# The order of a chunk's queries in the scores, and the gate of a batch's last 64 tokens on GpSimd

## The chip, the cores and the metric

One core of one Trainium2 chip. The time is device microseconds of one execution; before the change the median of three runs is 2122.11 us (2121.88 to 2122.24).

The engines, as the profile names them: PE is TensorE (matmuls; PEld its weight loads), DVE is VectorE, ACT is ScalarE, POOL is GpSimd, SP is SyncE, which issues the transfers.

## The reference

For each of 8 batches of 3136 tokens: scores of z with itself, rectified and squared, times v, gated by u; then of every batch the 128 tokens with the highest score against `w_gate` go through a small network (256 to 1024 to 256) and are added back with a sigmoid gate.

```python
scale = 1.0 / S                                       # S = 3136
scores = scale * np.matmul(z, z.transpose(0, 2, 1))   # z: 8 x 3136 x 64
attn = np.maximum(scores, 0.0) ** 2
x = u * np.matmul(attn, v)                            # u, v: 8 x 3136 x 256
gates = np.einsum('bsd,d->bs', x, w_gate)
top_idx = np.argpartition(-gates[b], capacity)[:capacity]       # capacity = 128
ye = np.maximum(xe @ w1, 0.0) @ w2
out[b, top_idx] = x[b, top_idx] + g[:, None] * ye               # g = sigmoid of the gate
```

## The kernel before

Everything is float32. To keep its precision on TensorE, an operand is split in a high part (rounded to fp32r) and a low part (the rest), and a product is high by high, high by low and low by high.

**Tiling.** A batch is cut in chunks of 512 queries (`CH`; six whole ones, `WHOLE`, and 64 tokens that are left, `REST`) and in tiles of 128 keys (`P`). A *slot* is a chunk with a pair of key tiles; slots of a batch and the batches stand one behind the other. For a new slot TensorE computes the scores (`scores`, L857): for each of the two key tiles a matmul with weights from `ZH` and one with weights from `ZL`, both with the moving operand `Z`, the chunk's 512 queries (high parts in partitions 0 to 63, low parts in 64 to 127). The result is the PSUM tile `sc`, in one of two rings. ACT rectifies it into `a` (`rise`) and squares it into the high part `hi` (`high`); VectorE or ACT squares `a` itself (`square`, and with that `sc` is free), and GpSimd or VectorE takes the low part `lo` = `a` - `hi` (`low`). Then `hi` and `lo` are the moving operands of the products with `V` (`multiply`), 8 matmuls with `hi` and 4 with `lo` in a slot, which add up in two PSUM banks of the chunk, `acc`, out of three.

**Symmetry.** Scores are symmetric, so a pair of a chunk and an earlier chunk's keys isn't computed again. VectorE transposes `a` in blocks of 32 x 32 (`turn`, `turn_own`), SyncE stores it in `squares` in HBM, and later fetches it into `qk` (`fetch`). Such an *old* slot (`old_scores`, L769) needs only a copy of the high part on ACT and the low part on GpSimd or VectorE. The slot on a chunk's diagonal takes half its columns from `own` (`half`, `fetch_own`), and its second score is 256 columns wide.

**The order of queries.** `ZH` and `ZL` hold z by tiles of 128 keys, in which the 512 tokens of a chunk stand as (t f a): t of 4 tiles, f of 4 groups, a of 32 tokens. The moving operand of the scores is the same data read as (f t a), so that it goes over the chunk in the order of its tokens: 16 runs of 32 elements, in the order of a view, not of memory:

```python
if c < WHOLE:
    Z[b, c] = t.rearrange("p (t f a) -> p f t a", t=GT, a=Q)
```

**A chunk's end.** When a chunk's last product is done, VectorE multiplies each accumulator by u (`evict` in `finish`) into `ut`, transposes it into `x`, SyncE stores it, GpSimd multiplies it by the gate weights and VectorE adds up the gates. The 64 tokens left over (`finish_rest`, L1208) end a batch: ACT and VectorE add three quarters of an accumulator in the tile `xr` (`lower`, `upper`, `total`), GpSimd multiplies by u (`product`), and VectorE weighs 2 x 32 tokens by the gate weights `w_bc` and adds the products up in one instruction each (`weigh`, `gate_of`, output `junk`).

**What sets the order.** The program is straight-line. While it is built, a planner with a clock model of each engine (`Clock`, `advance`, `choices`) puts the next piece of work on an engine: a `job` names the engines that may take it (`"pool|dve"`), a rank and what it needs. TensorE takes scores, then steps of the routing, then products, of what the model says is ready. So a change of a job's shape or engine moves instructions on all engines.

Of the kernel before, what the change touches and what calls it, by code (L numbers as in the profile page):

```python
# [18 lines left out]
P = 128  # L19
CH = 512  # L20
GT = 4
# [260 lines left out]
def attention_then_routed_ffn(ctx: ExitStack, tc: tile.TileContext, zt, ut, v, wg, w1, w2, cst, cst16, keys, outs, at, cap):  # L282
# [323 lines left out]
    def bring_z(b, c):  # L606

        c0, w = CHUNKS[c]
        t = moving_ring.take("Z", F32R)
        Z[b, c] = t[:, :w]  # L610
        for rows, z in ((slice(0, 64), ZH), (slice(64, P), ZL)):
            nc.sync.dma_start(t[rows, :w].bitcast(F32), z[rows, c0 : c0 + w].bitcast(F32))
        if c < WHOLE:
            Z[b, c] = t.rearrange("p (t f a) -> p f t a", t=GT, a=Q)

    def first_z():

        t = moving_ring.take("Z", F32R)
        Z[0, 0] = t.rearrange("p (t f a) -> p f t a", t=GT, a=Q)
# [129 lines left out]
    def fetch_own(b, c):  # L749
        ring = z_ring if c == 0 else v_ring  # L750
        st = ring.take("own", uses=2)
# [17 lines left out]
    def old_scores(k):  # L769
        b, c, js, _ = slots[k]  # L770
        g, t = js[0] // GT, js[0] % GT
        by = lambda x: x.rearrange("p q (f a) -> p q f a", a=Q)
        st = {}

        def high(e):
            src = fetched[b, c, g]
            st["src"] = src[:, :, t * Q : (t + 2) * Q].rearrange("p f (q a) -> p q f a", a=Q)
# [4 lines left out]
            job("pool|dve", k + 0.1, low, [st["src"], hi], [lo_ring], lambda: near(k), takes(2 * CH))  # L782

        def low(e):
            lo = lo_ring.take("lo", F32R)
            rest_on(e, by(lo), st["src"], by(parts[k][0]))
            parts[k][1], parts[k][3] = lo, True
            for _ in range(2):
                old_ring.drop(fetched[b, c, g])
# [31 lines left out]
    def own_rest(k, ps):  # L821
# [3 lines left out]
        def rise(e):  # L825
            a_.append(a_ring.take("a"))
            nc.scalar.activation(a_[0][:REST, 0, :REST], ps[:REST, 0, :REST], AF.Relu)
            job("act", k, high, [a_[0][:REST, 0, :REST]], (), lambda: "own_rest" in consts)

        def high(e):  # L830
            a = a_[0][:REST, 0, :REST]
            st = consts["own_rest"]
            nc.scalar.activation(st[:REST, :REST], a, AF.Square)
# [23 lines left out]
    def scores(k):  # L857
# [3 lines left out]
        if is_second(k):  # L861
            mov, w = mov[:, :, 2:], w // 2
# [15 lines left out]
        def rise(e):  # L878
            st["a_"] = a_ring.take("a")
            st["a"] = st["a_"][:, :n, :w]  # L880
            nc.scalar.activation(st["a"], ps, AF.Relu)
            job("act", k, high, [st["a"]], [hi_ring], lambda: near(k))

        def high(e):
# [5 lines left out]
            by = lambda x: x.rearrange("p q (f x) -> p q f x", x=P)  # L890
            if second:
                st["pieces"] = [(lambda x: by(x)[..., 64:], a.rearrange("p q (f x) -> p q f x", x=64))]
                nc.scalar.activation(st["pieces"][0][0](hi), st["pieces"][0][1], AF.Square)
# [7 lines left out]
        def half(e):  # L901
            src, ring, tile_ = fetched[b, c, c]
            hi = parts[k][0]
            by = lambda x: x.rearrange("p q (f x) -> p q f x", x=P)
            view = lambda x: by(x)[..., :64]
            src = src.rearrange("p f (q x) -> p q f x", q=2)
# [3 lines left out]
            job("pool|dve", k + 0.1, lambda e: low(e, view, src, lambda: ring.drop(tile_)), [src, view(hi)], took=takes(CH), rings=room, ok=turn_of)  # L910

        def square(e):
            a = st["a"]
            if e == "act":
                nc.scalar.activation(a, a, AF.Square)
# [22 lines left out]
        def low(e, view, src, after):  # L938
            if "lo" not in st:
                st["lo"] = lo_ring.take("lo", F32R)  # L940
                st["lows"] = 2 if second else 1
# [12 lines left out]
        def turn(q):  # L954
# [5 lines left out]
            nc.vector.transpose(to, a[rows, q].rearrange("p (m t a) -> p m t a", t=GT, a=Q))  # L960
# [25 lines left out]
        def turn_own(q):  # L986
# [5 lines left out]
            nc.vector.transpose(to, a[:, q].rearrange("p (m t a) -> p m t a", t=GT, a=Q)[:, :, 2:])  # L992
# [109 lines left out]
    def finish(b, c, h):  # L1102
# [106 lines left out]
    def finish_rest(b):  # L1209
# [14 lines left out]
        def upper(e):  # L1224
            s = st["s"]
            nc.vector.tensor_scalar(s, bank[:REST, D:], SCALE * SCALE, None, op0=ALU.mult)
            nc.vector.scalar_tensor_tensor(s, bank[:REST, :D], SCALE * SCALE, s, op0=ALU.mult, op1=ALU.add)
            drop_bank(bank)
            job("dve", rank + 2, total, [st["l"], s])

        def total(e):
            nc.vector.scalar_tensor_tensor(st["s"], st["l"], SCALE * SCALE, st["s"], op0=ALU.mult, op1=ALU.add)
# [993 lines left out]
```

## Time and profile before

| | us |
|---|---|
| median of 3 runs | 2122.11 |
| the profiled execution, its own time | 2121.96 |
| its span in the trace | 2119.8 |
| TensorE busy (matmuls) | 2090.4 (99%) |
| VectorE, ScalarE, GpSimd busy | 1387.1, 1346.5, 1374.7 (64 to 65%) |

The span is what the trace covers from the first instruction to the last; 2.2 us of the execution lie around it. Matmuls are pipelined: the record of one lasts some 390 ns, and the next begins after some 230, so the pace is read from the starts. The timeline view puts equal instructions that follow each other in one row, with the time of the first start.

### The profile page before, as it was taken

To read this page: it belongs to the slowest core of one execution; us is meant where nothing else is said; L and a number is where in the kernel's file an instruction comes from. 1 tells how busy PE (TensorE), PEld (TensorE's weight loads), DVE (VectorE), ACT (ScalarE), POOL (GpSimd) and SP (SyncE) were. 2 spreads that over 40 slices of the span, in tenths; PEclk is the share of its full clock that TensorE was granted. 3 is DMA by queue.
4 is the path that set the end of the run, shared out by engine and by line. 5 is a ranking of instruction groups with operands and counts; after the bars stand their busy time and mean duration, and the time that the engine had idled before them with its cause. 6 is when DMAs were issued, how large, how long until landed. Compare 5 with 4: busy or idle time off the path is not lost.

```text
span 2119.8 us, 28812 instructions
## 1 busy us (share of the span) xinstructions
PE 2090.4 (99%) x9317; PEld 1681.6 (79%) x9317; DVE 1387.1 (65%) x2216; ACT 1346.5 (64%) x1574; POOL 1374.7 (65%) x652
## 2 busy tenths in 40 slices
PE   8999999999999999999999999999999999999998
PEld 6888777887778877788777887778877888777777
DVE  6764587545875458754687446774467764787785
ACT  7766567655776557765676656766566665766642
POOL 6566766568665677656776568665676657755652
PEclk9999999999999999999999999999999999999999
DMA  7799667886678766787677876778767768667763
GB/s 212 213 256 256 171 189 207 248 214 168 184 215 252 206 159 204 222 255 195 159 202 218 263 185 171 201 222 253 185 172 207 205 180 198 182 194 198 213 156 93
DMA packets 426150, 428.37 MB, mean 202 GB/s; under 512 B 129040, under 2 KB 329360, under 8 KB 422416
## 3 DMA queue, kind: packets, MB, share of 16 engines
q1 hardware_dynamic: 425008, 424.18, 73.1%
q0 software_dynamic: 768, 2.10, 0.3%
q8 instruction: 73, 1.20, 0.2%
q14 instruction: 77, 0.63, 0.1%
q10 hardware_dynamic: 224, 0.26, 0.0%
HBM read 238.47 MB, written 175.37 MB: 195 GB/s over the span
## 4 chain that ended last, share of the span: by engine, by line
PE 69%; DMA 10%; SPq 6%; DVE 6%; issue 6%; ACT 2%; POOL 1%; POOLq 0%; ACTq 0%; DVEq 0%
PE acc L206 55%; PE sc L206 11%; SPq L206 6%; DMA squares<-aT 3%; DMA qk<-squares 2%; DMA squares_own<-aT 2%; DVE aT L206 2%; DMA vst<-in_v 2%; ACT hi L206 1%; DVE a L206 1%; DVE rest_hl L206 1%; ACT a L206 1%; PE y L206 1%; PE h L206 1%; DVE lo L206 1%
## 5 line engine op out<-in xcount | busy, mean ns | idle before, releaser
L206 PE MATMUL acc<-hi,V 128*128 128x512 f32 x4800 | 1226.4, 393 | 6.8 <-ACT hi L206 4.6
L206 PEld LDWEIGHTS acc<-hi,V 128*128 128x128 f32 x4800 | 893.1, 188 | 201.1 <-ACT hi L206 8.7
L206 POOL TENSOR_TENSOR lo<-a,hi 128x1024 fp32r<-128x1024 f32 (+1 forms) x243 | 584.4, 2406 | 389.1 <-ACT a L206 270.6
L206 PE MATMUL acc<-lo,V 128*128 128x512 f32 x2304 | 636.4, 393 | 0.0
L206 DVE STREAM_TRANSPOSE aT<-a 128x512 f32<-128x512 f32 (+2 forms) x622 | 381.4, 647 | 296.4 <-ACT a L206 204.1
L206 ACT ACTIVATE a<-sc 128x1024 f32<-128x1024 f32 (+1 forms) x392 | 353.9, 903 | 257.3 <-PE sc L206 71.8
L206 PEld LDWEIGHTS acc<-lo,V 128*128 128x128 f32 x2304 | 429.3, 188 | 91.5 <-POOL lo L206 2.6
L206 POOL TENSOR_TENSOR lo<-qk,hi 128x1024 fp32r<-128x1024 f32 x166 | 416.3, 2508 | 105.4 <-ACT hi L206 88.2
L206 ACT ACTIVATE hi<-a 128x1024 fp32r<-128x1024 f32 (+1 forms) x384 | 366.4, 955 | 153.1 <-PE acc L206 137.2
L206 ACT CAST hi<-qk 128x1024 fp32r<-128x1024 f32 x240 | 250.8, 1048 | 190.6 <-PE acc L206 157.7
L206 PE MATMUL sc<-Z,ZH 128*128 128x512 f32 (+1 forms) x728 | 280.1, 388 | 13.7 <-DVE a L206 9.8
L206 PE MATMUL sc<-Z,ZL 128*128 128x512 f32 (+1 forms) x728 | 275.1, 381 | 0.6 <-POOL ZL L206 0.6
L206 ACT ACTIVATE a<-a 128x1024 f32<-128x1024 f32 x237 | 251.4, 1061 | 6.7
L206 DVE TENSOR_TENSOR a<-sc,a 128x1024 f32<-128x1024 f32 (+3 forms) x155 | 129.9, 838 | 99.9 <-ACT hi L206 77.9
L206 PEld LDWEIGHTS sc<-Z,ZH 128*128 128x128 f32 x728 | 136.9, 188 | 57.2 <-DVE a L206 18.1
L206 DVE TENSOR_TENSOR lo<-a,hi 128x1024 fp32r<-128x1024 f32 (+1 forms) x93 | 141.1, 1518 | 32.5 <-ACT a L206 28.3
L206 PEld LDWEIGHTS sc<-Z,ZL 128*128 128x128 f32 x728 | 138.2, 190 | 29.7 <-POOL ZL L206 0.9
L206 POOL TENSOR_TENSOR ut<-x,w_run 128x1024 f32<-128x1024 f32 x45 | 129.6, 2881 | 34.0 <-DVE x L206 34.0
L206 DVE TENSOR_TENSOR lo<-qk,hi 128x1024 fp32r<-128x1024 f32 x74 | 132.4, 1789 | 21.4 <-ACT hi L206 14.7
L206 POOL TENSOR_TENSOR V<-vst,V 128x512 fp32r<-128x512 f32 (+1 forms) x67 | 85.7, 1285 | 75.9 <-ACT V L206 75.4
L206 DVE SCALAR_TENSOR_TENSOR ut<-acc,ut 128x512 f32<-128x512 f32 x96 | 63.4, 681 | 77.5 <-PE acc L206 77.2
L206 DVE TENSOR_TENSOR V<-vst,V 128x512 fp32r<-128x512 f32 x37 | 57.5, 1569 | 51.1 <-ACT V L206 51.1
(195 smaller groups left out, 1163.5 us busy)
## 6 DMA issues: line engine op xcount, KB each, us to landing
squares<-aT SPq DMA_DIRECT2D x240, 512.0 KB, 4.5
qk<-squares SPq DMA_DIRECT2D x480, 256.0 KB, 6.1
ut<-in_ut SPq DMA_DIRECT2D x48, 512.0 KB, 5.4
vst<-in_v SPq DMA_DIRECT2D x191, 128.0 KB, 3.3
out<-x SPq DMA_DIRECT2D x188, 128.0 KB, 3.6
squares_own<-aT SPq DMA_DIRECT2D x47, 256.0 KB, 2.0
own<-squares_own SPq DMA_DIRECT2D x188, 64.0 KB, 3.1
zst<-in_zt SPq DMA_DIRECT2D x85, 128.0 KB, 6.8
```

The source lines that it names most:

```text
L206: got = real(*args, **kw)
```

## The change

The scores' moving operand is read as it lies, in the order of z's key tiles (`bring_z`, `first_z`). All that comes from scores is then in the order (t f a), and it is put back where it is used otherwise: the transposes read `a` in the other order (`turn`, `turn_own`), old slots and the diagonal's half put the fetched columns in the new order, and the eviction reads the accumulator through a view. The second score of the diagonal takes the last 256 columns as one run. The low part of an old slot is taken in two instructions of 512 columns (`for q in range(2)`), the diagonal's in two of 256.

The factor `SCALE * SCALE` of the eviction moves into the relu, and the squares get `1 / SCALE`.

For the last 64 tokens, `total` and `product` go to GpSimd, `weigh` becomes one product of 64 x 256 on GpSimd, and VectorE adds up 2 x 32 tokens (`add`). The last batch keeps its own way for this (`column`).

```diff
@@ bring_z, first_z
-        if c < WHOLE:
-            Z[b, c] = t.rearrange("p (t f a) -> p f t a", t=GT, a=Q)
-        Z[0, 0] = t.rearrange("p (t f a) -> p f t a", t=GT, a=Q)
+        Z[0, 0] = t
@@ old_scores
+            st["left"] = 2
+            for q in range(2):
+                room = lambda: () if parts[k][1] else (lo_ring,)
+                job("pool|dve", k + 0.1, lambda e, q=q: low(e, q), [st["src"], hi], room, lambda: parts[k][1] or near(k), takes(CH))
-            job("pool|dve", k + 0.1, low, [st["src"], hi], [lo_ring], lambda: near(k), takes(2 * CH))
@@ scores
-            mov, w = mov[:, :, 2:], w // 2
+            mov, w = mov[:, w // 2 :], w // 2
-            nc.scalar.activation(st["a"], ps, AF.Relu)
+            nc.scalar.activation(st["a"], ps, AF.Relu, scale=SCALE * SCALE)
-                nc.scalar.activation(hi, a, AF.Square)
+                nc.scalar.activation(hi, a, AF.Square, scale=1 / SCALE)
@@ half
+            for q in range(2):
+                job("pool|dve", k + 0.1, lambda e, q=q: low(e, lambda x: view(x)[:, q], src[:, q], lambda: ring.drop(tile_)), [src, view(hi)], took=takes(CH // 2), rings=room, ok=turn_of)
@@ turn
-            nc.vector.transpose(to, a[rows, q].rearrange("p (m t a) -> p m t a", t=GT, a=Q))
+            nc.vector.transpose(to, a[rows, q].rearrange("p (t m a) -> p m t a", t=GT, a=Q))
@@ finish: evict
-            nc.vector.scalar_tensor_tensor(
-                xT[:, h], acc[b, c, h], SCALE * SCALE, xT[:, h], op0=ALU.mult, op1=ALU.mult
-            )
+            to, src = xT[:, h], acc[b, c, h]
+            if c < WHOLE:
+                to = to.rearrange("p (f t a) -> p f t a", t=GT, a=Q)
+                src = src.rearrange("p (t f a) -> p f t a", t=GT, a=Q)
+            nc.vector.tensor_tensor(to, src, to, op=ALU.mult)
@@ finish_rest
-            job("dve", rank + 2, total, [st["l"], s])
+            job("pool" if scored else "dve", rank + 2, total, [st["l"], s])
-            job("pool|dve" if scored else "dve", rank + 2, product, [st["s"]], took=takes(D), ok=lambda: b in turned_u)
+            job("pool" if scored else "dve", rank + 2, product, [st["s"]], ok=lambda: b in turned_u)
-                for i in range(2):
-                    job("dve", rank + 6, lambda e, i=i: weigh(i), [st["x"]])
+                job("pool", rank + 6, weigh, [st["x"]])
-        def weigh(i):
+        def weigh(e):
+            nc.gpsimd.tensor_tensor(st["s"], st["x"], consts["wg"][:REST], op=ALU.mult)
+            for i in range(2):
+                job("dve", rank + 8, lambda e, i=i: add(i), [st["s"]])
+
+        def add(i):
-            gate_of(st["x"][at_], gate[b][at_, o : o + 1], at_)
+            nc.vector.tensor_reduce(gate[b][at_, o : o + 1], st["s"][at_], axis=AX.X, op=ALU.add)
```

VectorE at the end of the second batch, from the first instruction on `xr` on. Before (`junk` is the gate product, `a<-sc,a` the square that frees a score bank, `ut<-acc,ut` the eviction):

```order
L206 TENSOR_SCALAR xr<-acc 64x256
L206 SCALAR_TENSOR_TENSOR xr<-acc,xr 64x256
L206 SCALAR_TENSOR_TENSOR xr<-xr 64x256
L206 TENSOR_TENSOR lo<-qk,hi 128x1024
L206 SCALAR_TENSOR_TENSOR junk,gate<-xr,w_bc 32x256
L206 TENSOR_TENSOR V<-vst,V 128x512
L206 SCALAR_TENSOR_TENSOR junk,gate<-xr,w_bc 32x256
L206 STREAM_TRANSPOSE aT<-a 128x8x32 x2
L206 TENSOR_TENSOR a<-sc,a 128x1024
L206 SCALAR_TENSOR_TENSOR ut<-acc,ut 128x512
```

And now:

```order
L206 COPY xr<-acc 64x256
L206 TENSOR_TENSOR xr<-acc,xr 64x256
L206 TENSOR_TENSOR lo<-qk,hi 128x512 x3
L206 TENSOR_TENSOR ZL<-zst,ZH 128x4x4x32
L206 TENSOR_TENSOR V<-vst,V 128x512
L206 STREAM_TRANSPOSE aT<-a 128x8x32 x2
L206 TENSOR_TENSOR ut<-acc,ut 128x512
L206 TENSOR_TENSOR lo<-a,hi 128x1024
L206 TENSOR_TENSOR ut<-acc,ut 128x512
L206 STREAM_TRANSPOSE aT<-a 128x4x128 x2
L206 TENSOR_REDUCE gate<-xr 32x1
```

The two gate products are gone from ahead of the square and the eviction; three halves of `lo<-qk` and a `ZL` stand there, and the first sum of the gate comes behind the evictions.

GpSimd at the same place. Before:

```order
L206 TENSOR_TENSOR rest_hl<-rest,rest_hl 128x8x64
L206 TENSOR_TENSOR lo<-a,hi 128x8x64
L206 TENSOR_TENSOR xr<-xr,rest_u 64x2x4x32
L206 TENSOR_TENSOR lo<-qk,hi 128x1024
L206 TENSOR_TENSOR ZL<-zst,ZH 128x4x4x32
L206 TENSOR_TENSOR V<-vst,V 128x512
L206 TENSOR_TENSOR lo<-a,hi 128x1024
```

And now:

```order
L206 TENSOR_TENSOR rest_hl<-rest,rest_hl 128x8x64
L206 TENSOR_TENSOR lo<-a,hi 128x2x256
L206 TENSOR_TENSOR xr<-xr 64x256
L206 TENSOR_TENSOR lo<-qk,hi 128x512
L206 TENSOR_TENSOR lo<-own,hi 128x256 x2
L206 TENSOR_TENSOR xr<-xr,rest_u 64x2x4x32
L206 TENSOR_TENSOR V<-vst,V 128x512
L206 TENSOR_TENSOR lo<-a,hi 128x1024
L206 TENSOR_TENSOR xr<-xr,w_bc 64x256
```

Two instructions on `xr` are new there, and three stand in a chain with other work between them.

TensorE at the same place, from the last two matmuls of the new chunk's second score to the third score. Before:

```order
L206 MATMUL sc<-Z,ZH 128x512
L206 MATMUL sc<-Z,ZL 128x512
L206 MATMUL acc<-hi,V 128x512 x8
L206 MATMUL acc<-lo,V 128x512 x4
L206 MATMUL sc<-Z,ZH 128x512
```

And now:

```order
L206 MATMUL sc<-Z,ZH 128x512
L206 MATMUL sc<-Z,ZL 128x512
L206 MATMUL acc<-lo,V 128x512 x4
L206 MATMUL sc<-Z,ZH 128x512
L206 MATMUL sc<-Z,ZL 128x512
```

The third score follows the second after 4 products in place of 12; between the third and the fourth there are 12 in both.

In the whole program, instructions that take the low part, by engine:

| | GpSimd before | now | VectorE before | now |
|---|---|---|---|---|
| `lo<-qk`, 1024 columns | 166 | 0 | 74 | 0 |
| `lo<-qk`, 512 columns | 0 | 261 | 0 | 219 |
| `lo<-a`, 1024 columns | 228 | 199 | 61 | 90 |

## Rows read from the trace of the kernel before

**Rows 1.** The page: the span, and each engine's busy time and share.

```profile
span 2119.8 us, 28812 instructions
...
PE 2090.4 (99%) x9317; PEld 1681.6 (79%) x9317; DVE 1387.1 (65%) x2216; ACT 1346.5 (64%) x1574; POOL 1374.7 (65%) x652
```

**Rows 2.** TensorE's groups by shape: xcount | busy us, mean ns | idle us.

```profile
L206 PE MATMUL acc<-hi,V 128*128 128x512 f32 x4800 | 1226.4, 393 | 6.8 <-ACT hi L206 4.6 <-DVE hi L206 1.9
L206 PE MATMUL sc<-Z,ZH 128*128 128x512 f32 x626 | 254.0, 406 | 13.7 <-DVE a L206 9.8 <-ACT a L206 3.4 <-DVE Z L206 0.5
L206 PE MATMUL sc<-Z,ZL 128*128 128x512 f32 x626 | 248.5, 397 | 0.6 <-POOL ZL L206 0.6
...
L206 PE MATMUL h<-wl,xh 128*128 128x512 f32 x24 | 7.5, 395 | 0.0
```

**Rows 3.** Timeline, TensorE, 1001 to 1012 us: start us, us, instruction, xcount.

```profile
1001.71 1.98 PE L206 MATMUL acc<-hi,V 128*128 128x512 f32 x8
1003.52 1.08 PE L206 MATMUL acc<-lo,V 128*128 128x512 f32 x4
...
1008.58 0.40 PE L206 MATMUL sc<-Z,ZH 128*128 128x512 f32 x1
...
1009.52 1.99 PE L206 MATMUL acc<-hi,V 128*128 128x512 f32 x8
1011.35 0.84 PE L206 MATMUL acc<-lo,V 128*128 128x512 f32 x3
```

**Rows 4.** Timeline of TensorE where an expert's first layer runs, 416 to 418 us.

```profile
416.31 0.62 PE L206 MATMUL h<-wh,xh 128*128 128x512 f32 x2
...
417.70 1.09 PE L206 MATMUL acc<-hi,V 128*128 128x512 f32 x4
```

**Rows 5.** Waits of TensorE: us in total, times, longest us.

```profile
PE sc L206 <- DVE a L206: 9.8, 14, 1.1
```

**Rows 6.** VectorE's groups by shape: the last 64 tokens' gate.

```profile
L206 DVE SCALAR_TENSOR_TENSOR junk<-xr,w_bc 32x256 f32<-32x256 f32 x14 | 53.3, 3808 | 4.6 <-POOL xr L206 4.4
```

**Rows 7.** Timeline of all engines at the second batch's end, 519 to 530 us.

```profile
519.36 5.11 DVE L206 SCALAR_TENSOR_TENSOR junk<-xr,w_bc 32x256 f32<-32x256 f32 x1 [0.64 <-POOL xr L206]
...
524.21 3.15 POOL L206 TENSOR_TENSOR lo<-a,hi 128x1024 fp32r<-128x1024 f32 x1
524.48 1.06 ACT L206 ACTIVATE hi<-a 128x1024 fp32r<-128x1024 f32 x1
...
525.12 2.52 DVE L206 SCALAR_TENSOR_TENSOR junk<-xr,w_bc 32x256 f32<-32x256 f32 x1
...
527.88 0.61 PE L206 MATMUL acc<-lo,V 128*128 128x512 f32 x2
...
528.35 1.19 DVE L206 TENSOR_TENSOR a<-sc,a 128x1024 f32<-128x1024 f32 x1
...
529.59 0.50 PE L206 MATMUL sc<-Z,ZH 128*128 128x512 f32 x1 [1.10 <-DVE a L206]
```

**Rows 8.** Groups by line and shape, VectorE (DVE), then GpSimd (POOL).

```profile
L206 DVE TENSOR_TENSOR lo<-qk,hi 128x1024 fp32r<-128x1024 f32 x74 | 132.4, 1789 | 21.4 <-ACT hi L206 14.7 <-DMA qk<-squares 3.6 <-issue 2.9
L206 DVE TENSOR_TENSOR lo<-a,hi 128x1024 fp32r<-128x1024 f32 x61 | 94.7, 1553 | 29.6 <-ACT a L206 28.3 <-issue 1.1
L206 DVE SCALAR_TENSOR_TENSOR ut<-acc,ut 128x512 f32<-128x512 f32 x96 | 63.4, 681 | 77.5 <-PE acc L206 77.2
...
L206 DVE TENSOR_REDUCE gate<-ut 128x16 f32<-128x1024 f32 x45 | 54.3, 1207 | 42.0 <-POOL ut L206 42.0
L206 DVE TENSOR_TENSOR lo<-a,hi 128x512 fp32r<-128x512 f32 x32 | 46.4, 1451 | 2.9
...
L206 DVE TENSOR_TENSOR a<-sc,a 128x512 f32<-128x512 f32 x47 | 32.2, 686 | 55.7 <-ACT hi L206 55.2 <-issue 0.5
...
L206 POOL TENSOR_TENSOR xr<-xr,rest_u 64x256 f32<-64x256 f32 x7 | 11.6, 1655 | 16.7 <-DVE xr L206 16.7
...
L206 POOL TENSOR_TENSOR V<-vst,V 128x256 fp32r<-128x256 f32 x8 | 5.9, 737 | 30.7 <-ACT V L206 30.7
```

More of the change, by code (lines that the diff above doesn't have):

```diff
@@ L750, in fetch_own @@
         ring = z_ring if c == 0 else v_ring
-        st = ring.take("own", uses=2)
+        st = ring.take("own", uses=3)
         t = st if c == 0 else st.rearrange("p a d -> p (a d)")[:, :CH]
@@ L781, in high, with low @@
             parts[k][2] = True
-            job("pool|dve", k + 0.1, low, [st["src"], hi], [lo_ring], lambda: near(k), takes(2 * CH))
[L784 to L789, printed above, removed]
+            st["left"] = 2
+            for q in range(2):
+                room = lambda: () if parts[k][1] else (lo_ring,)
+                job("pool|dve", k + 0.1, lambda e, q=q: low(e, q), [st["src"], hi], room, lambda: parts[k][1] or near(k), takes(CH))
+        def low(e, q):
+            if parts[k][1] is None:
+                parts[k][1] = lo_ring.take("lo", F32R)
+            rest_on(e, by(parts[k][1])[:, q], st["src"][:, q], by(parts[k][0])[:, q])
+            st["left"] -= 1
+            parts[k][3] = st["left"] == 0
+            old_ring.drop(fetched[b, c, g])
         here = lambda: (b, c, g) in fetched
@@ L903, in half @@
             hi = parts[k][0]
-            by = lambda x: x.rearrange("p q (f x) -> p q f x", x=P)
-            view = lambda x: by(x)[..., :64]
-            src = src.rearrange("p f (q x) -> p q f x", q=2)
+            view = lambda x: x[:, :, :w].rearrange("p q (t f a) -> p q t f a", t=2, a=Q)
+            src = src.rearrange("p f (q t a) -> p q t f a", q=2, a=Q)
             nc.scalar.copy(view(hi), src)
@@ L909, in half @@
             parts[k][2] = True
-            job("pool|dve", k + 0.1, lambda e: low(e, view, src, lambda: ring.drop(tile_)), [src, view(hi)], took=takes(CH), rings=room, ok=turn_of)
+            for q in range(2):
+                job("pool|dve", k + 0.1, lambda e, q=q: low(e, lambda x: view(x)[:, q], src[:, q], lambda: ring.drop(tile_)), [src, view(hi)], took=takes(CH // 2), rings=room, ok=turn_of)
         def square(e):
@@ L940, in low @@
                 st["lo"] = lo_ring.take("lo", F32R)
-                st["lows"] = 2 if second else 1
+                st["lows"] = 3 if second else 1
             rest_on(e, view(st["lo"]), src, view(parts[k][0]))
@@ L1225, in upper @@
             s = st["s"]
[L1226 to L1227 removed]
+            nc.vector.tensor_copy(s, bank[:REST, D:])
+            nc.vector.tensor_tensor(s, bank[:REST, :D], s, op=ALU.add)
             drop_bank(bank)
[L1229 removed]
+            job("pool" if scored else "dve", rank + 2, total, [st["l"], s])
         def total(e):
[L1232 to L1233 removed]
+            ON[e].tensor_tensor(st["s"], st["l"], st["s"], op=ALU.add)
+            job("pool" if scored else "dve", rank + 2, product, [st["s"]], ok=lambda: b in turned_u)
         def product(e):
```

17 lines of the change are left out of this document (8 added, 9 removed).

## The prediction

> **What bounds the kernel now.** I read the page's engine line first: TensorE is busy for 2090.4 of 2119.8 us, and VectorE, ScalarE and GpSimd for 64 to 65% [rows 1]. So only two things can move the end by more than a microsecond or two: how fast TensorE goes from one matmul to the next, and the little time in which it waits. The busy share itself hides the first, since matmuls overlap in the records; so the second view is the timeline of TensorE, where the distance of starts is the pace. Eight product matmuls (acc) in an undisturbed stretch take 1001.71 to 1003.52, 1.81 us, 0.226 each. Four score matmuls (sc) of the same 512 columns take 1008.58 to 1009.52, 0.94 us, 0.235 each. And the eight products behind them take 1009.52 to 1011.35, 1.83 us, a little more than eight that follow products [rows 3]. The groups say the same: a mean of 393 ns for acc, 406 and 397 for the two halves of a score, whose moving operand is read in 16 runs of 32 elements [rows 2]. The third view is the table of waits: TensorE's dearest one is for VectorE's tile a, 9.8 us in 14 times, the longest 1.1 us [rows 5].
>
> **Part 1, the scores' moving operand becomes contiguous.** There are 626 + 626 score matmuls of 512 columns [rows 2] (and 188 of 256 columns, left out of the sum). What would a contiguous one cost? Two rows bound it. If it became like an undisturbed product, it would take 0.226 us, and the slower products behind a score would go too: four scores and the eight products behind them take 1008.58 to 1011.35, 2.77 us, against 12 x 0.226 = 2.715 [rows 3]. That is 0.055 us for four scores, 13.75 ns for one, and 1252 x 13.75 ns = 17 us. The other end is the nearest row of matmuls that are already contiguous, 512 columns wide, and stand alone between others as the scores do: the six h matmuls of an expert, 416.31 to 417.70, 1.39 us, 0.232 each [rows 4]. They are no faster than the products that follow scores, though they read one run. So a disturbance of the pace comes with leaving the products' tiles, not with runs alone; only 0.235 - 0.232 = 0.003 us is then the runs' share, 1252 x 0.0033 = 4 us. By the groups' means (406 and 397 against h's 395 [rows 2]) it is 626 x 11 ns + 626 x 2 ns = 8 us, but those means hold modelled ends. I take 5 us, near the h rows, because h matmuls are what a contiguous score will look like; the ends are 0 and 17 us. A loss has no row for it: no contiguous 512-column group stands slower than the scores.
>
> Here the Trainium skill speaks against the change: its page "SBUF — State Buffer", in "Door 1: The DMA port swizzle", says that SBUF is read in lines of 16 bytes and that only steps from line to line cost, so four fp32 in a row are enough. By that rule a run of 32 elements is whole lines and its stride is free, and this part would bring 0 instead of 5 us; the 0.235 against 0.226 speaks against it, the 0.232 of h for it.
>
> **Part 2, the gate products of the last 64 tokens.** In 7 of the 8 batches (all but the last) VectorE multiplies 32 x 256 elements twice by the gate weights, with an instruction that reads two SBUF tiles. These 14 records have a mean of 3808 ns and 53.3 us in all [rows 6]. For 256 columns that is not work but waiting: one of them takes 5.11 us from 519.36, another 2.52 us from 525.12, and GpSimd is busy through both, with the row of 3.15 us at 524.21 among others [rows 7]. Behind them on VectorE stands the square of the new chunk's second score (its row at 528.35), whose input, ACT's hi, had been there since 524.48 + 1.06 = 525.54; it frees the score bank that TensorE wants at 528.49: the wait is 1.10 us at 529.59, and the record of the matmul after it is 0.50 us long where the scores' others have 0.40 [rows 3, 7]. The cost is 1.10 + 0.10 = 1.2 us in a batch, 7 x 1.2 = 8.4 us; 7 x 1.1 = 7.7 of the 9.8 us of [rows 5] are these, the other 7 waits have 0.3 us each and stay.
>
> The change moves that product to GpSimd and leaves VectorE two sums over 32 x 256, which read one tile: by the 1207 ns of a sum over 1024 columns [rows 8] 0.3 us each, with no GpSimd to wait for. What is late next? Without that waiting the square can run from 525.54 to 526.75, 1.7 us before TensorE asks. The order of the change has thinner cover at that place: the second and third scores of the new chunk are only four products apart (the rows under "The change"), so from the end of the second to the start of the fourth there are 4 + 4 + 12 matmuls = 4.6 us, and relu, hi and square of the second take 3 x 1.06 = 3.2 us if ACT takes them at once. I count 7.5 of the 8.4 us as gone. The ends are 0 (another late step takes the place) and 8.4.
>
> GpSimd gets two new instructions of 64 x 256 in a batch. Its rows bound one: 737 ns for 128 x 256 unit-stride elements, 1655 ns for the permuted product of the same 64 tokens [rows 8]; so 1.5 to 3.3 us in a batch, 10 to 23 us in all. What is queued behind them there are low parts (lo) and V's; TensorE's idle time before matmuls that read lo does not appear among its waits, and GpSimd is idle for 35% of the span [rows 1]. I take 0 on the path.
>
> **Part 3, halves in place of wholes.** The low part of an old slot (lo<-qk) is now two instructions of 512 columns, since its view has too many dimensions for one. The changed program has 261 of them on GpSimd and 219 on VectorE, in place of 166 and 74 wholes, and VectorE gets 29 more wholes of lo<-a (90 for 61). A half on VectorE costs between 0.69 us (a 512-column product that reads PSUM) and 1.45 us (one that reads two SBUF tiles beside GpSimd) [rows 8], so 219 cost 151 to 318 us for the 132 of the wholes; 29 wholes of lo<-a at 1.55 us [rows 8] make 45, and the gate's 53 go. That is 11 to 178 us more on an engine with 733 us idle [rows 1]. GpSimd has 29 wholes of lo<-a less and the work of 35 wholes of lo<-qk less. Cover for the lows is the lead of three slots with which they are made; none of TensorE's waits today is for one. I take 0, and the end against it is a rival.
>
> **Part 4, the rest has one answer.** Scaling moves from the eviction into the relu and the square: no instruction more. The eviction of a chunk, 681 ns from PSUM with three operands, becomes a product like a<-sc with 686 ns [rows 8], with a permuted view; if the view doubled it, 96 x 0.68 us would lie on VectorE behind a chunk's end, where three banks serve two accumulators. ACT's copies and VectorE's 32 x 32 transposes read the same runs in another order. One more idle matmul at the end: under 0.3 us.
>
> **Sum.** Against the profiled run's own 2121.96 us (its span of 2119.8 and 2.2 us around it; the median of the runs, 2122.11, is 0.15 us above it): 2121.96 - 5 - 7.5 = 2109.5 us.
>
> **The rivals.**
> A: the pace falls into the products' 0.226 all through. For it: products keep 0.226 over changes of bank and tile among themselves. Against it: h, contiguous and still at 0.232. Then 2122 - 17 - 7.5 = 2097.5 us (2092 to 2102).
> B: the 0.235 comes whole from leaving the products' tiles, as h's 0.232 does, and the runs cost nothing; the gate part works: 2122 - 7.5 = 2114.5 us (2112 to 2118). The rule of the Trainium skill's page "SBUF — State Buffer" on lines would have it so. It is also the case in which the change of order does not do what it says.
> C: the gate's wait is replaced by one for ACT or for GpSimd, which now carries three dependent steps of the 64 tokens between lows, or for the eviction behind VectorE's halves: 2122 - 5 = 2117 us if all 7.5 us come back that way, and 2122 us if the runs are free besides. For it: the thinner cover of part 2.
> D, slower: VectorE's 219 halves and 90 wholes each wait for a running GpSimd instruction, as the gate's did, and squares and evictions come late behind them. Each such delay costs 1.2 us [rows 7]; the gain of 12.5 us is used up by 10 of them, and 14 make the kernel slower by over 0.2%. With two in each of the 8 batches it is 16 x 1.2 = 19 us, 2128.5 us. Against it: today's 74 + 61 wholes of that kind cause only the 7 waits of 0.3 us.
>
> **How the numbers follow.** The forecast (2104 to 2113) gets 0.45, A 0.20, B 0.13, C 0.14, D 0.08. A difference of 0.2% (4.2 us, about what a measurement of this kernel can tell from no change) begins below 2117.9. Faster: 0.45 + 0.20 + 0.12 of B + 0.03 of C = 0.80; same: 0.01 + 0.11 = 0.12; slower 0.08. The range from 2092 to 2119 holds the forecast, A, B and a third of C; D and most of C are outside, 0.18.
>
> **What would show it.** Part 1: in the timeline of the changed kernel, four scores between products take 0.93 us (right), 0.905 (A) or 0.94 (B); sc's means come to 395, or 393 in A. Part 2: no record above 1 us on VectorE for the 64 tokens' gate, and the wait of sc for VectorE's a falls from 9.8 to about 2 us. Part 3: no wait of acc for lo, and VectorE's busy time between 1390 and 1570 us. What would make it wrong: a pace that follows neither row, or new waits at the batch ends of over 1 us.

## The result

The changed kernel takes 2102.84 us (median of 4 runs, 2100.16 to 2103.44) against 2121.99 us for the kernel before (4 runs): a ratio of 0.9901, 95% interval 0.9889 to 0.9913. On another chip it was 2101.67 against 2123.27 us, 0.9900 (0.9883 to 0.9916). So it is faster by 19.2 us, about 1%. The forecast was 2109.5 us, 12.5 us faster, in a range from 2092 to 2119: the sign and the range held, but the time lies just below the band that the forecast itself was given (2104 to 2113), and the gain was half as large again as the sum.

The profiled run took 2102.34 us, its span 2100.2 us. The page's busy line, which answers to [rows 1]:

```profile
span 2100.2 us, 29357 instructions
...
PE 2077.3 (99%) x9318; PEld 1682.2 (80%) x9318; DVE 1454.9 (69%) x2348; ACT 1362.8 (65%) x1584; POOL 1369.1 (65%) x790
```

TensorE has 13 us less of busy time for the same products and scores, VectorE 68 us more. The groups of TensorE by shape, which answer to [rows 2] (records, busy us and mean ns of one, idle time ahead and what ended it):

```profile
L206 PE MATMUL acc<-hi,V 128*128 128x512 f32 x4800 | 1222.3, 393 | 5.2 <-ACT hi L206 4.0 <-DVE hi L206 0.4
...
L206 PE MATMUL sc<-Z,ZL 128*128 128x512 f32 x626 | 246.3, 394 | 0.6 <-POOL ZL L206 0.6
L206 PE MATMUL sc<-Z,ZH 128*128 128x512 f32 x626 | 246.1, 393 | 0.2 <-DVE Z L206 0.2
```

The scores' means fell from 406 and 397 to 393 and 394 ns, and the 13.7 us of idle time ahead of them are 0.2. The waits of TensorE (us in total, times, the longest):

```profile
PE acc L206 <- POOL lo L206: 8.8, 13, 1.1
PE acc L206 <- ACT hi L206: 4.0, 2, 2.9
...
PE idle L206 <- DVE hl L206: 1.2, 1, 1.2
PE acc L206 <- DVE lo L206: 0.7, 1, 0.7
...
PE sc L206 <- ACT a L206: 0.2, 1, 0.2
```

The wait of the scores for VectorE's a, 9.8 us in [rows 5], has no row any more. In its place there is a new one, 8.8 us for low parts made on GpSimd. Six of its 13 times, 4.0 us, are at batch ends. Six more, 4.6 us, stand some 43 us behind those; near there the kernel before had its waits of scores for ACT's a, 3.4 us in [rows 2]. The second of those at batch ends, in the timeline of GpSimd, TensorE and VectorE (start us, us, instruction), and the wait that follows it:

```profile
512.08 0.69 DVE L206 TENSOR_TENSOR lo<-qk,hi 128x512 fp32r<-128x512 f32 x1
...
512.14 1.24 POOL L206 TENSOR_TENSOR xr<-xr 64x256 f32<-64x256 f32 x1 [2.58 <-ACT hi L206]
...
513.34 1.30 POOL L206 TENSOR_TENSOR lo<-qk,hi 128x512 fp32r<-128x512 f32 x1
...
514.59 2.32 POOL L206 TENSOR_TENSOR lo<-own,hi 128x256 fp32r<-128x256 f32 x2
...
515.82 0.74 PE L206 MATMUL acc<-lo,V 128*128 128x512 f32 x2 [0.68 <-POOL lo L206]
...
525.68 0.36 DVE L206 TENSOR_REDUCE gate<-xr 32x1 f32<-32x256 f32 x1
...
558.49 1.20 PE L206 MATMUL acc<-lo,V 128*128 128x512 f32 x4 [0.40 <-POOL lo L206]
```

TensorE alone, right behind it:

```profile
517.79 0.40 PE L206 MATMUL sc<-Z,ZH 128*128 128x512 f32 x1
...
518.71 1.09 PE L206 MATMUL acc<-lo,V 128*128 128x512 f32 x4
```

GpSimd adds the two parts of the last 64 tokens (1.24 us, the new xr<-xr) ahead of the low parts that TensorE waits for at 515.82. That addition begins 0.06 us behind a half of a low part on VectorE, which reads two SBUF tiles (512.08), and is long for its size: GpSimd's two other instructions of 64 x 256 at this batch end take 0.74 and 0.73 us. Four scores take 517.79 to 518.71, 0.92 us, 0.230 each, where [rows 3] had 0.94. The sum that was left to VectorE of the gate takes 0.36 us, where [rows 7] had records of 5.11 and 2.52.

### The profile page after: what moved, and what is told of

It is laid out like the page before. It is cut to its first block, busy times and chain, and to the rows that moved or that the text cites. A ratio compares the mean times of both kernels' runs of the same rounds, so it can differ in the third digit from the quotient of the medians.

```text
span 2100.2 us, 29357 instructions
## 1 busy us (share of the span) xinstructions
PE 2077.3 (99%) x9318; PEld 1682.2 (80%) x9318; DVE 1454.9 (69%) x2348; ACT 1362.8 (65%) x1584; POOL 1369.1 (65%) x790
## 4 chain that ended last, share of the span: by engine, by line
PE 82%; DVE 5%; issue 4%; DMA 3%; SPq 2%; POOL 2%; ACT 2%; POOLq 0%; DVEq 0%; ACTq 0%
PE acc L206 68%; PE sc L206 11%; SPq L206 2%; DMA vst<-in_v 2%; POOL lo L206 1%; DMA squares<-aT 1%; DVE aT L206 1%; DVE lo L206 1%; ACT a L206 1%; ACT hi L206 1%; PE y L206 1%; PE h L206 1%; DVE a L206 0%; DVE beats L206 0%; DVE mk L206 0%
## 5 line engine op out<-in xcount | busy, mean ns | idle before, releaser
L206 POOL TENSOR_TENSOR lo<-a,hi 128x1024 fp32r<-128x1024 f32 (+1 forms) x215 | 505.6, 2352 | 366.7 <-ACT a L206 225.2
L206 POOL TENSOR_TENSOR lo<-qk,hi 128x512 fp32r<-128x512 f32 x261 | 422.6, 1627 | 161.8 <-ACT hi L206 151.8
L206 DVE TENSOR_TENSOR lo<-qk,hi 128x512 fp32r<-128x512 f32 x219 | 249.1, 1142 | 144.4 <-ACT hi L206 125.6
L206 PE MATMUL sc<-Z,ZH 128*128 128x512 f32 (+1 forms) x728 | 272.2, 377 | 0.4 <-ACT a L206 0.2
L206 ACT ACTIVATE a<-a 128x1024 f32<-128x1024 f32 x247 | 262.2, 1062 | 7.2
L206 DVE TENSOR_TENSOR lo<-a,hi 128x1024 fp32r<-128x1024 f32 (+1 forms) x121 | 181.0, 1496 | 44.8 <-ACT a L206 20.1
L206 DVE TENSOR_TENSOR a<-sc,a 64x512 f32<-64x512 f32 (+3 forms) x145 | 117.5, 811 | 61.6 <-ACT hi L206 55.3
L206 POOL TENSOR_TENSOR V<-vst,V 128x512 fp32r<-128x512 f32 (+1 forms) x62 | 94.0, 1522 | 27.3 <-ACT V L206 21.3
L206 POOL TENSOR_TENSOR lo<-own,hi 128x256 fp32r<-128x256 f32 x93 | 83.5, 918 | 29.2 <-ACT hi L206 23.0
L206 DVE TENSOR_TENSOR ut<-acc,ut 128x512 f32<-128x512 f32 x96 | 63.7, 684 | 49.0 <-PE acc L206 48.5
```

Source lines behind the costliest of these rows:

```text
L206: got = real(*args, **kw)
```

## The experiments

Theory T is that of the prediction with its two terms: contiguous scores are worth some 5 us, and the gate product of VectorE that waits for GpSimd some 7.5 to 8.4 us. Since 19.2 us came, one of the two is too small, or the halves and the new order gain something themselves. The rivals are B (the runs cost nothing), A (the pace becomes 0.226 everywhere) and C (waits are replaced by others). Each ratio below is against the kernel before in runs on the same chip.

### What the runs of 32 cost

**e1_runs32**: the changed kernel, the scores read in 16 runs again (here for `bring_z`; likewise in `first_z` and for the diagonal's second score).

```
+        if c < WHOLE:
+            Z[b, c] = t.rearrange("p (t f a) -> p f t a", t=GT, a=Q)
```

> The changed kernel, with its scores' moving operand read in 16 runs of 32 elements again; every engine's order stays as it is, and the scores' columns come out in another order than the rest takes them for. If the runs themselves cost the pace (the scores' own and that of the products behind them), this is slower than the changed kernel by what the two traces' distances of starts differ by at scores and the products next to them, 10 to 13 us: 2113 to 2116 us. If the change's gain came mostly from the new order of work, with the runs worth the 5 us of the prediction, it takes about 2108 us. If the runs are free, 2103 us.

Measured: 2109.45 us, 0.9932 (0.9916 to 0.9949), 0.31% or 6.6 us above the changed kernel's ratio. Four scores take 1032.75 to 1033.69, 0.94 us again, as before:

```profile
1032.75 0.40 PE L206 MATMUL sc<-Z,ZH 128*128 128x512 f32 x1
...
1033.69 3.15 PE L206 MATMUL acc<-hi,V 128*128 128x512 f32 x12
```

**e2_contig_before**: the other way round, the kernel before with the contiguous read alone (its view of Z left as it lies, in the three places where it was turned).

> The kernel before, with its scores' moving operand read as it lies and nothing else changed: every engine's order is the same as before, and the scores' columns come out in another order than the rest takes them for. If the runs cost the pace, it gains 10 to 13 us whatever the order of work: 2109 to 2112 us. With the prediction's 5 us it takes 2117 us; with free runs 2122 us.

Measured: 2117.18 us, 0.9972 (0.9963 to 0.9982), so 5.9 us less (3.8 to 7.9). The runs cost something, and B falls; they do not cost 17 us, and A falls. Both kernels agree on 6 us. The pace itself gained more than the end did. Summed over all records, the distance from one score of 512 columns to the next start was 10.5 us more in the kernel before than at 226.67 ns each (the products' commonest distance), and is 4.2 us more here; the products' sum fell from 14.65 to 12.1 us (distances over 250 ns left out). That is 8.8 us of pace. Part of it comes back as waits for engines that are now reached earlier: the waits of scores for VectorE's a are 10.7 us here against 9.8 [rows 5]. e1_runs32 shows the same from the other side: with the slower scores its wait for GpSimd's lo is 5.8 us, against 8.8 in the changed kernel.

**e6_runs8** and **e7_runs2**: what is it in a run that costs? The changed kernel with its scores read in 64 runs of 8 elements, and in 256 runs of 2.

```
-        Z[0, 0] = t
+        Z[0, 0] = t.rearrange("p (t f a) -> p f t a", t=8, a=8)      e7: t=16, a=2
```

> The changed kernel with the scores' moving operand read in 64 runs of 8 elements (32 bytes) instead of one run; the queries of a chunk then come in another order than the later steps take them, so the outputs are not the reference's, and every step is the same work. 16 runs cost 6.6 us in e1_runs32. Theory 1, each run costs its own time: four times as much, 26 us, 2129 us. Theory 2, any operand in more than one run costs the same: 2109 us. Theory 3, only steps within a run matter (elements one after another are free): 2103 to 2109 us, and the next kernel tells more.

> As e6_runs8, with 256 runs of 2 elements (8 bytes). Theory 1, each run costs its own time: 16 times the 6.6 us of 16 runs, 105 us, 2208 us. Theory 2, any operand in more than one run costs the same: 2109 us. The rule of the Trainium skill (page 'SBUF — State Buffer', 'Door 1: The DMA port swizzle') on lines of 16 bytes would make runs of 8 bytes dearer than runs of 32: by it e6_runs8 stays at or under 2109 us and only this kernel is slower.

Measured: 2122.79 us for runs of 8 (0.9997, 0.9988 to 1.0007), 20 us above the changed kernel, and 2389.64 us for runs of 2 (1.1254), 287 us above. Both rules are too simple. Timeline of TensorE in e6_runs8, then in e7_runs2:

```profile
1040.90 0.41 PE L206 MATMUL sc<-Z,ZH 128*128 128x512 f32 x1
...
1041.90 2.95 PE L206 MATMUL acc<-hi,V 128*128 128x512 f32 x12
```

```profile
530.43 0.62 PE L206 MATMUL sc<-Z,ZH 128*128 128x512 f32 x1
...
532.22 2.06 PE L206 MATMUL acc<-hi,V 128*128 128x512 f32 x8
```

Four scores take 1.00 us in 64 runs of 8 and 1.79 us in 256 runs of 2, against 0.94 in 16 runs of 32 and 0.92 in one. From one run to 64 that is 0.02 us a score, 0.3 ns a run, and from one to 16 it is 0.005 us, again 0.3 ns a run: down to 8 elements each run costs its own time (theory 1 of the two expectations). By that price 256 runs would cost 0.08 us a score; they cost (1.79 - 0.92) / 4 = 0.22. The Trainium skill, "SBUF — State Buffer", "Door 1: The DMA port swizzle", says that SBUF is read in lines of 16 bytes, that two hits in a line are needed for full bandwidth, and that one may step over 4 fp32 for free. Lines of that size fit e7_runs2: a run of 2 uses half a line, and a score takes 0.45 us, about double. That two hits are enough doesn't fit it. And runs of 8 and of 32 fill whole lines, so that they cross into new ones no oftener than a single run does, and still cost more. The end follows the pace, less what the waits give back: e6_runs8 has 5.4 us of waits for lo instead of 8.8.

### What VectorE's product with two SBUF inputs costs

**e8_gate_one_input**: the order of the kernel before, its gate of the last 64 tokens without the weights in 7 batches.

```
-            gate_of(st["x"][at_], gate[b][at_, o : o + 1], at_)
+            nc.vector.tensor_reduce(to, x, axis=AX.X, op=ALU.add)
```

> The kernel before, in its own order, with the gate of the last 64 tokens of 7 batches summed without the weights (that product is left out), so that VectorE's instruction reads one SBUF tile in place of two. If VectorE waited there for GpSimd, its records fall from 3808 to about 300 ns, the 7 waits of TensorE for the score bank go, and the kernel gains 7 x 1.2 = 8.4 us: 2113.6 us. If another late step takes the place of that wait, it takes 2118 to 2122 us.

Measured: 2109.57 us, 0.9936 (0.9919 to 0.9952): 13.3 us less, not 8.4. The orders are the same, so the starts of the same matmul can be subtracted, the kernel before minus this one. At the second batch's end of the kernel before, TensorE's timeline goes 527.88 (two products), 529.59 (the first score) [rows 7], and then

```profile
529.93 0.40 PE L206 MATMUL sc<-Z,ZL 128*128 128x512 f32 x1
```

In e8_gate_one_input the same three rows are

```profile
525.57 0.62 PE L206 MATMUL acc<-lo,V 128*128 128x512 f32 x2
526.03 0.40 PE L206 MATMUL sc<-Z,ZH 128*128 128x512 f32 x1
526.27 0.40 PE L206 MATMUL sc<-Z,ZL 128*128 128x512 f32 x1
```

From the products to the first score it was 1.71 us and is 0.46, and the next score follows after 0.24 instead of 0.34: 1.35 us, where the prediction had 1.2. It had added the wait of 1.10 and 0.10 for a longer record; but the wait counts from 528.49, the end of a record which in an undisturbed stretch overlaps the next start by 0.15. Seven such steps, of 1.33 to 1.35 us, are 9.4 us. The rest of the 14.25 us between the two profiled runs lies elsewhere: 0.20 us at two scores 7.6 us behind each step, 1.4 us in all; four differences of 0.22 to 0.67 us some 30 to 40 us behind such a step, 1.9 us in all (one is a wait of a score for ACT's a, 0.78 us at 562.11 in the kernel before); 0.94 us ahead of the last batch's products, and smaller ones of both signs. How these hang on the gate was not traced. Its waits for VectorE's a, 9.8 us in [rows 5]:

```profile
PE sc L206 <- DVE a L206: 1.9, 6, 0.3
```

**e12_two_inputs**: the undo in the changed kernel, with nothing else moved (the planner's records of the old steps are kept here, in e8_gate_one_input, e9_no_total and e11_fold_total, so that its order stands).

```
-            nc.gpsimd.tensor_tensor(st["s"], st["x"], consts["wg"][:REST], op=ALU.mult)
-            nc.vector.tensor_reduce(gate..., st["s"][at_], axis=AX.X, op=ALU.add)
+            nc.vector.scalar_tensor_tensor(st["s"][at_], st["x"][at_], 1.0, consts["wg"][at_], ..., accum_out=to)
```

> The changed kernel, with the gate product of the last 64 tokens taken back from GpSimd: VectorE's two sums of 32 x 256 become two multiply-and-sums that read two SBUF tiles, in the places where the sums stood; all other instructions stand where they stood. Theory 1, the VectorE instruction that reads two SBUF tiles waits out GpSimd's running one, and the square behind it comes late: the 7 waits of the kernel before come back, at most the 13.3 us that e8_gate_one_input gave; since the places differ from before's (a 2.4 us GpSimd instruction begins just ahead of the first sum, 525.46 against 525.68), 5 to 13 us, 2108 to 2116 us. Theory 2, in the changed order the square has room, and the delay is hidden: 2102 to 2104 us.

Measured: 2116.14 us, 14.5 us above the changed kernel on the same chip (2101.67), at the upper end of theory 1's times and 1.2 us over the 13.3 us that it allowed for. The mechanism stands in its timeline, in the group of the products and in the waits of TensorE for VectorE's a:

```profile
529.64 2.40 POOL L206 TENSOR_TENSOR lo<-a,hi 128x1024 fp32r<-128x1024 f32 x1 [3.33 <-ACT a L206]
...
529.82 2.50 DVE L1270 SCALAR_TENSOR_TENSOR xr<-xr,w_bc 32x256 f32<-32x256 f32 x1
...
532.70 1.29 POOL L206 TENSOR_TENSOR V<-vst,V 128x512 fp32r<-128x512 f32 x1 [0.65 <-ACT V L206]
...
533.58 0.69 DVE L1270 SCALAR_TENSOR_TENSOR xr<-xr,w_bc 32x256 f32<-32x256 f32 x1
...
534.95 1.19 DVE L206 TENSOR_TENSOR a<-sc,a 128x1024 f32<-128x1024 f32 x1
...
536.19 0.50 PE L206 MATMUL sc<-Z,ZH 128*128 128x512 f32 x1 [1.31 <-DVE a L206]
...
1831.06 0.37 DVE L1270 SCALAR_TENSOR_TENSOR xr<-xr,w_bc 32x256 f32<-32x256 f32 x1
```

```profile
L1270 DVE SCALAR_TENSOR_TENSOR xr<-xr,w_bc 32x256 f32<-32x256 f32 x14 | 20.0, 1426 | 0.2
```

```profile
PE sc L206 <- DVE a L206: 7.9, 6, 1.3
```

By starts of the same matmul, this kernel minus the changed one, there are six steps at the batch ends, 1.47 us at the score that waits and 1.6 us with the matmuls beside it, 9.7 us; and again 0.28 to 0.75 us in six places 25 to 30 us behind them, 3.3 us in all. Another 2.0 of the 15.1 us between the two profiled runs lie in the first 180 us, ahead of any batch end, and so aren't the gate's: some 13 us are, as in e8_gate_one_input.

The product begins 0.18 us behind a GpSimd instruction and ends 0.28 us behind its end. The next one begins while GpSimd is at V (532.70) and takes 0.69 us; it too ends 0.28 us behind GpSimd (534.27 against 533.99). Only in the seventh batch is GpSimd idle beside the product: there it takes 0.37 us (1831.06), and TensorE has no such wait. One long hold in a batch is enough: the 14 records have 20.0 us here against 53.3 in [rows 6], and the price at the end is no lower. What counts is how late the square (534.95) is, not how long the product stood.

### Whether GpSimd's addition makes the new wait

**e9_no_total**: the changed kernel without that addition in the 7 batches.

```
-            ON[e].tensor_tensor(st["s"], st["l"], st["s"], op=ALU.add)
+            (left out where e is "pool")
```

> The changed kernel, in its own order, without the sum of the last 64 tokens' third quarter on GpSimd in 7 batches (that addition is left out). If this instruction, which stands ahead of a low part, is what made the low part late that TensorE waits for at each batch's end (0.68 us of idle time in the second batch, 0.85 us between starts), then 7 such waits go and the kernel gains 5 to 6 us: 2097 us. If the low parts in halves are late by themselves, the waits stay and it takes 2102 to 2103 us.

Measured: 2099.43 us, 0.9881 (0.9864 to 0.9897), 0.2% or some 4 us under the changed kernel's ratio. That could still be the missing dependence, so the addition was next made in another place:

**e11_fold_total**: VectorE adds ScalarE's part while it takes the bank out of PSUM.

```
-            nc.vector.tensor_copy(s, bank[:REST, D:])
+            nc.vector.tensor_tensor(s, bank[:REST, D:], st["l"], op=ALU.add)
             nc.vector.tensor_tensor(s, bank[:REST, :D], s, op=ALU.add)
-            (total) ON[e].tensor_tensor(st["s"], st["l"], st["s"], op=ALU.add)
```

> The changed kernel, with the addition of the last 64 tokens' parts folded into the step ahead of it: VectorE adds one PSUM bank's half to what ScalarE had copied (in place of a copy out of PSUM) and then the other half, so that GpSimd's separate addition (64 x 256, 1.2 us, once a batch) is gone and no VectorE instruction is added. All other instructions stand where they stood. ScalarE's copy ends before VectorE's step begins (510.73 + 0.37 against 511.13 in the changed kernel's timeline). Theory 1, GpSimd's addition ahead of the low parts makes TensorE wait at the 7 batch ends: the waits of acc for lo fall from 8.8 to about 4 us as in e9_no_total, and the time is 2099 to 2100 us, 3 to 4 us below the changed kernel on the same chip. Theory 2, what e9_no_total gained came from leaving the data dependence out: level with the changed kernel, within 1 us.

Measured: 2098.42 us (2098.07 to 2099.15), 0.9886 (0.9870 to 0.9903), against 2101.67 us (2100.20 to 2103.53) for the changed kernel beside it: all its runs lie under all of the other's. At the same batch end GpSimd now goes straight to the half, and the products behind wait for nothing:

```profile
512.91 1.81 POOL L206 TENSOR_TENSOR lo<-qk,hi 128x512 fp32r<-128x512 f32 x1 [2.57 <-ACT hi L206]
...
514.68 2.33 POOL L206 TENSOR_TENSOR lo<-own,hi 128x256 fp32r<-128x256 f32 x2
...
515.92 0.74 PE L206 MATMUL acc<-lo,V 128*128 128x512 f32 x2
```

```profile
PE acc L206 <- POOL lo L206: 3.7, 5, 1.2
PE sc L206 <- DMA Z<-ZL: 1.6, 1, 1.6
```

By starts of the same matmul, the changed kernel minus this one, six steps of 0.51 to 0.67 us at the batch ends make 3.8 us; against them stands 1.7 us at 178 us, where a wait for a transfer of Z comes up, and smaller gains make the 4.3 us between the two profiled runs. So theory 1 holds, and this version beats both kernels, by 3.3 and 24.9 us. None of the five waits for lo that are left is at a batch end; four stand some 43 us behind one, and what makes those low parts late was not tested.

**e5_total_dve**: the same addition handed to VectorE as a step of its own, with the planner free to move what follows.

```
-            job("pool" if scored else "dve", rank + 2, total, [st["l"], s])
+            job("dve", rank + 2, total, [st["l"], s])
```

> The changed kernel with one step of the last 64 tokens put back on VectorE: the addition of the two parts (64 x 256, one instruction a batch). GpSimd then no longer holds it ahead of the low parts at the 7 batch ends; the planner's order of some later steps moves with it. Theory 1, that addition is what makes TensorE wait for lo at the batch ends: the 7 waits go as they did in e9_no_total, and the time is 2099 to 2100.5 us. Theory 2, the VectorE instruction reads two SBUF tiles and waits for GpSimd as the old gate product did, and the squares behind it come late: 7 x 0.5 to 1.2 us come back, 2103 to 2108 us.

Measured: 2124.42 us, 1.0003 (0.9992 to 1.0014): the whole gain is gone, far outside both theories. Its waits of TensorE, then TensorE and ScalarE some 35 us behind the second batch's end, and the clock in three stretches (length, PE busy, records, granted clock as a share of full speed, DMA share, GB/s):

```profile
PE acc L206 <- ACT V L206: 9.0, 6, 1.5
PE acc L206 <- POOL lo L206: 7.7, 12, 0.8
```

```profile
551.96 1.02 ACT L206 ACTIVATE a<-sc 128x1024 f32<-128x1024 f32 x1 [6.29 <-DVE aT L206]
...
553.04 0.50 PE L206 MATMUL sc<-Z,ZH 128*128 128x512 f32 x1 [0.86 <-ACT a L206]
...
555.07 1.12 ACT L206 CAST V<-vst 128x512 fp32r<-128x512 f32 x2
...
555.73 1.18 PE L206 MATMUL acc<-hi,V 128*128 128x512 f32 x4 [1.49 <-ACT V L206]
...
557.73 1.56 PE L206 MATMUL acc<-lo,V 128*128 128x512 f32 x3 [0.80 <-POOL lo L206]
```

```profile
556.00:558.00 2.00, 1.20 (x6) 0.96 0.39 138
558.00:561.00 3.00, 3.00 (x10) 0.50 0.06 19
561.00:565.00 4.00, 4.00 (x18) 0.97 0.65 228
```

In the new order ScalarE's V stands behind a relu that waits 6.29 us for VectorE; TensorE stops for 0.86, 1.49 and 0.80 us within 6 us, and right behind these stops the granted clock is 0.50, the lower of its two levels (1.2 GHz), for 3 us. Such a place costs 3.9 to 4.9 us, in five batches (starts of equal matmul numbers, this kernel minus the changed one, over 60 matmuls from the first stop on). In the first batch the same three stops (291.50, 294.19, 296.19) are not followed by a lower clock, and the place costs 2.7 us. The six places together, 25 us, are more than the 21.9 us between the profiled runs. So the price lies at these places of the other order: this kernel doesn't tell what the addition alone costs on VectorE.

### Whether the two parts are the whole

**e10_both**: the kernel before with both edits (e2_contig_before and e8_gate_one_input).

> The kernel before with two edits alone: the scores' moving operand read in one run (as in e2_contig_before) and the gate sums of the last 64 tokens in 7 batches without their weights, so that VectorE's instruction there reads one SBUF tile (as in e8_gate_one_input; that gate is then a plain sum of the row). No halves of lo<-qk, no GpSimd steps, no other order. Theory 1, the two parts explain the whole gain and add: 2122 - 5.9 - 13.3 = 2103 us, level with the changed kernel's 2102.8. Theory 2, the two gains overlap (both end in waits for the same late steps): 2106 to 2109 us. Theory 3, the halves and the new order of the changed kernel cost something that its gain hides (its waits for GpSimd's lo, 8.8 us): then this kernel is faster than the changed one, 2098 to 2100 us.

Measured: 2107.18 us (2101.58, 2105.29, 2109.06, 2109.55), 0.9927 (0.9910 to 0.9945). The profiled run, 2101.58 us, is level with the changed kernel, the median 4 us above it. The two longest runs had a mean granted clock of 0.996 and 0.997, the others 0.999: by that alone they are some 6 and 4 us longer (an estimate: 0.003 and 0.002 of 2107 us), and without it all four would lie between 2101 and 2106 us. Only one run has a trace. Theory 3 falls; between 1 and 2 it stays open, with 1 the nearer after that estimate. The undos in the changed order, 6.6 and 14.5 us, make 21.1 us together, near the whole of 19.2 to 21.6; so the halves and the new order are worth nothing on balance that these intervals (some 4 us each) could tell. They do cost something, 3.3 us by e11_fold_total, and gain something: in e10_both TensorE's scores still wait for ACT and VectorE,

```profile
PE sc L206 <- ACT a L206: 4.8, 6, 1.1
...
PE sc L206 <- DVE a L206: 2.2, 7, 0.3
```

which in the changed kernel are 0.2 us and nothing; there the six other waits for lo, 4.6 us, stand near their place.

**after_again**: the changed kernel beside e11_fold_total and e12_two_inputs.

> The changed kernel once more, on the chip of the two others, as what they stand against: 2102 to 2104 us.

Measured: 2101.67 us, as told at the top.

## Why the prediction was right, and where its size was off

- **What bounds it.** Right: TensorE's pace and its few waits were the places to look. Both moved: from the one profiled run to the other, distances of up to 250 ns between the 512-column products and scores gained 9.7 us and the longer ones 10.6, which is the whole of the 19.6 us within 1 us.
- **Part 1**, 5 us: right in size, 5.9 and 6.6 us in the two experiments. The h rows were the right neighbour: a score now takes 0.230 us, near their 0.232 [rows 4], not the products' 0.226. About half of the disturbance stays with a contiguous operand, and the runs came on top of it; that the rest comes with leaving the products' tiles, as the prediction says, was not tested. Not seen was that the pace gives 8.8 us and waits take 2 to 3 us back. Of the two marks set for it the timeline's held (0.92 us, nearest to 0.93), and the means pointed the wrong way: 393 and 394 ns were to stand for rival A. The record ends are modelled, and the distance of starts decides.
- **Part 2**, 7.5 of 8.4 us: this is the term that was mis-sized. The mechanism was right in each step (the held product, the late square, the bank that TensorE wants), and it measured 13.3 us in the old order and 14.5 us in the new. Two things were missing. A wait of the view starts at the end of the record ahead, which overlaps the next start by 0.15 us: 1.35 us, not 1.2, in a batch. And 2 to 3 us lie some 25 to 40 us behind the late squares, where no row at the batch end shows them; that they hang on the gate is known by subtraction alone. The 0.9 us that were kept back from the 8.4 had no row. In the changed kernel the seven small waits of 0.3 us that were to stay, and most of the 3.4 us of scores for ACT's a [rows 2], are gone too, with the six waits for lo near their place.
- **GpSimd's two new instructions**, 0 on the path: wrong, by 3.3 us. The prediction took it from 35% of idle time and from the lack of waits for lo; but at a batch end GpSimd is the last to finish, and 1.24 us ahead of the low parts there are 0.54 to 0.70 us of wait on TensorE, six times. The table of waits of the kernel before had a sign of it that the prediction passed over, a wait for another low part that GpSimd makes there, once in a batch:

```profile
PE acc L206 <- POOL rest_hl L206: 2.6, 7, 1.2
```

Their own time, 1.22 and 0.74 us, lies within the bounds given. The addition is the longer one in the six batches where it begins 0.06 us behind VectorE's low part, so some 0.5 us of it may be a hold like the gate's, the other way round; no run tests that. The weighing product (5.2 us in 7 times) shows no wait of its own. This is rival C's mechanism, at under half of its 7.5 us.

- **Part 3**, 0 on the path and VectorE busy for 1390 to 1570 us: 1454.9 us, with 219 halves of 1142 ns. Rival D did not come: VectorE's low parts are read by TensorE late enough for one wait of 0.7 us, no square is late behind them. That no wait of acc for lo would show was wrong, for the reason above at six batch ends, and for one that stays open at six other places. Two halves on GpSimd, which were one record of 2508 ns, now take 1627 ns each (groups by shape, as [rows 8]):

```profile
L206 POOL TENSOR_TENSOR lo<-qk,hi 128x512 fp32r<-128x512 f32 x261 | 422.6, 1627 | 161.8 <-ACT hi L206 151.8 <-DMA squares_last<-aT 3.8 <-DMA qk<-squares 2.8
...
L206 DVE TENSOR_TENSOR lo<-qk,hi 128x512 fp32r<-128x512 f32 x219 | 249.1, 1142 | 144.4 <-ACT hi L206 125.6 <-issue 10.7 <-DMA qk<-squares 4.0
```

- **Part 4**, 0: nothing in the waits answers to the permuted eviction or to the scaling. But the one more idle matmul at the end, under 0.3 us in the prediction, stands in an order in which it waits for VectorE:

```profile
2082.20 0.35 PE L206 MATMUL idle<-c 128*128 128x418 bf16 x1 [1.18 <-DVE hl L206]
```

From the first matmul that writes `lent` (2091.31 before, 2070.24 now) to the end of the span it is 29.9 us in place of 28.5, with no other matmul added: 1.4 us that the change loses.

- **The sum** with the measured terms: 2122 - 6 - 14 + 3.3 + 1.4 is some 2107 us, against 2102.3 in the profiled run; the 4 to 5 us left are about the interval of one undo (4 us), and the waits of scores that the new order took away would fill them. That the range held although one term was half of what it measured and another was put at 0 is in part luck: the range was wide enough for rival A, which did not come. Of the rivals, A and B fell by e1_runs32 and e2_contig_before, D by the waits; C came in part.

## What to carry to other kernels

Price a stall by the distance of starts with and without it and by what it makes late behind it, not by the wait row alone: here the row said 7.7 us and the end gained 13 to 14. An instruction that is moved to an idle engine is free only if that engine isn't the last to finish at that very place; an average of idle time says nothing on that. And look whether a small step can be folded into one that must run anyway, as the addition was.

## What was unexpected of the hardware

- A moving operand of 512 fp32 columns costs about 0.3 ns for each run of 8 to 32 elements (0.92, 0.94 and 1.00 us for four matmuls in 1, 16 and 64 runs), and about twice the time in runs of 2 (1.79 us).
- Three stops of TensorE within 6 us, 0.86, 1.49 and 0.80 us, were followed by 3 us at half the clock in five batches of e5_total_dve and not in a sixth. There the place costs 2.7 us in place of 3.9 to 4.9, so neighbouring waits can be dearer than their sum. Of single stops, one of 1.83 us at 47.65 in after_again was followed by it, one of 1.86 us at 2043.86 in the kernel before was not; the stops of 1.1 us [rows 5] were not either: in that trace every stretch of 10 us behind the first 20 has 1.00.
- In e12_two_inputs VectorE's product of two SBUF tiles ended 0.27 to 0.28 us behind GpSimd's running instruction in all 12 records that had one beside them, and took 0.37 and 0.41 us in the two that had none.
